# A wait for VectorE in front of each GpSimd operation on their shared port

## The chip, the core and the metric

The kernel runs on one NeuronCore of a Trainium2 chip. The core has five engines that run side by side, each through its own instruction queue in program order: TensorE (PE in the profile, its weight loads PEld), VectorE (DVE), ScalarE (ACT), GpSimd (POOL) and SyncE (SP), which here only starts DMA transfers. Engines wait for one another through semaphores. TensorE reads SBUF and writes PSUM; VectorE and ScalarE reach both memories; GpSimd works on SBUF alone. The metric is the device time of one launch in microseconds (us), lower being better.

## The reference

Eight batches, twelve heads, 448 tokens, head size 64. Attention uses a sigmoid in place of a softmax; its output, with the heads side by side, is the input of a gated linear layer whose gate is a causal convolution of five taps.

```python
scores = scale * np.matmul(q, k.transpose(0, 1, 3, 2)) - np.log(S)
attn = 1.0 / (1.0 + np.exp(-scores))
x = np.matmul(attn, v)                    # then (B, S, 768)
for k in range(5):
    gate_pre += conv_w[k][None, None, :] * xp[:, k:k + S, :]
gate = 1.0 / (1.0 + np.exp(-gate_pre))
out = gate * (x @ w_val) @ w_out
```

## The kernel before, in words

All results must be good to float32, so most operands are split in two: a high part in a narrow type and a low part, which is the source minus the high part. Three matmuls (high by high, low by high, high by low) then stand for one.

*Attention.* Heads are taken in 48 pairs. A pair's q and k arrive in one tile `qk_src` [128, 896]. Two copies (L387 on VectorE or L385 on ScalarE) make `qk_hi`, two subtractions on GpSimd make `qk_lo` (`split_qk`, through the helper `sub`, L396). Scores go to PSUM (`scores`, L560; the leftover rows L583), ScalarE takes the sigmoid (L596) and the scaled high part `a` (L391), VectorE the low part (`a`, `a_rest`, L607, read from PSUM). The product with v (`v_hi`, L393, and `v_lo`, L627) is L646 and L654. The first pairs run as plain float32 without splits.

*Gate.* The attention output `x` is scaled and split into `xs` (L393 high, L785 low). The taps are multiplied on ScalarE or VectorE (L391, L393, L723) and some are summed by DMAs that GpSimd issues and that add into `gate` (L727). ScalarE takes the sigmoid (L729).

*The two linear layers.* `product("val")` multiplies `xs` by the weights (L984), VectorE joins the gate (L994, L1004). For the later batches the second layer is done with one level of a fast matrix product: `mix` makes sums and differences of weight blocks (`mix`, `mixed`; L396, L806, L812, L814, L823), `form` makes sums of blocks of the gated values (four additions in place, L861, then high and low parts, L387 and L396), and `product_mixed` runs the smaller products (L921) and collects them in `y` (L934).

*Order.* Every operation is an `Op` with a list of engines that may do it, the tiles it reads and writes, and a mark `port`: the default `"VG"` says that it uses the SBUF port shared by VectorE and GpSimd when it runs on either; `port=""` says that it does not (operations that read PSUM, reductions, memsets, and the DMAs that GpSimd issues). The table `ORDER` lists all 2724 operations in one sequence, the string `ENGINES` gives one letter to each (P, V, A, G or S). `plan.issue()` reads the two and the last loop emits the operations in that sequence, so each engine's queue holds its own operations in the order of the table. Between engines only data and buffers make anyone wait: nothing in the kernel before holds a GpSimd operation until a VectorE operation that stands ahead of it in the table has run, unless it reads or overwrites a tile of that operation.

On GpSimd the table puts 97 operations with the port mark (60 subtractions for `qk_lo`, the rest in `mix`, `form` and two for `g`), 60 DMA issues and 24 memsets without it.

Of the kernel before, what the change touches and what calls it, by code (L numbers as in the profile page):

```python
# [278 lines left out]
def attention_then_gate(  # L279
# [20 lines left out]
    nc = tc.nc  # L300
# [755 lines left out]
    def rest(j):  # L1056
        o = scores_rest(j)
        t = tau(2 * j) + AT["a_rest_first" if 2 * j < AHEAD else "a_rest"]
        two[j]["a_next"] = lambda: attention(two[j], t, two[j]["ps"], rest_ring, "a_rest", j in WHOLE)
        return o  # L1060
# [5 lines left out]
    for j in range(TWOS):  # L1066
# [10 lines left out]
        else:  # L1077
            o = rest(j + 1) if j + 1 < TWOS else None
# [49 lines left out]
    product_mixed(B - 2, range(NQ - HELD, NQ), AT["held"])  # L1128
    product_mixed(B - 1)
    plan.close(rings)  # L1130
    for o in plan.issue():
        o.emit(o.eng)


# [47 lines left out]
```

## Time and profile before

| | |
|---|---|
| time, median of 3 runs | 587.87 us (587.75 to 588.45) |
| the profiled execution | 586.95 us, its span 585.1 us |
| TensorE busy | 564.8 us, 97% of the span |
| VectorE busy | 502.0 us, 86% |
| ScalarE busy | 453.7 us, 78% |
| GpSimd busy | 187.8 us, 32% (208 instructions) |
| chain of waits, by engine | PE 63%, DVE 27%, ACT 5% |

The span runs from the first to the last instruction; the time has some 1.9 us around it. A busy TensorE is not TensorE at its peak, since matmuls overlap and their ends are modelled. The chain of waits is followed back from the last instruction, at each step to what released it.

### The profile page before, as it was taken

To read this page: it belongs to the slowest core of one execution; us is meant where nothing else is said; L and a number is where in the kernel's file an instruction comes from. 1 tells how busy PE (TensorE), PEld (TensorE's weight loads), DVE (VectorE), ACT (ScalarE), POOL (GpSimd) and SP (SyncE) were. 2 spreads that over 40 slices of the span, in tenths; PEclk is the share of its full clock that TensorE was granted. 3 is DMA by queue.
4 is the path that set the end of the run, shared out by engine and by line. 5 is a ranking of instruction groups with operands and counts; after the bars stand their busy time and mean duration, and the time that the engine had idled before them with its cause. 6 is when DMAs were issued, how large, how long until landed. Compare 5 with 4: busy or idle time off the path is not lost.

```text
span 585.1 us, 10537 instructions
## 1 busy us (share of the span) xinstructions
PE 564.8 (97%) x4043; PEld 323.5 (55%) x4043; DVE 502.0 (86%) x814; ACT 453.7 (78%) x609; POOL 187.8 (32%) x208
## 2 busy tenths in 40 slices
PE   9999999899989898899999999999999999999996
PEld 4343334344544456565557754467655775456685
DVE  2778999999999999998999999998789886994633
ACT  5688687797979998898999997998958987673220
POOL 0000122534527544325672412432323313112410
PEclk9999999999999999999999999999999999999999
DMA  8689767936364645667555754667755454535114
GB/s 323 266 256 320 279 138 173 241 57 176 77 162 105 152 123 107 180 151 180 134 147 119 195 122 110 158 146 162 176 138 127 118 120 105 109 72 109 37 37 145
DMA packets 40081, 88.50 MB, mean 151 GB/s; under 512 B 14944, under 2 KB 21216, under 8 KB 40032
## 3 DMA queue, kind: packets, MB, share of 16 engines
q1 hardware_dynamic: 31392, 56.37, 29.4%
q0 software_dynamic: 8640, 31.46, 28.7%
q8 instruction: 32, 0.52, 0.4%
q14 instruction: 17, 0.14, 0.1%
HBM read 43.96 MB, written 12.40 MB: 96 GB/s over the span
## 4 chain that ended last, share of the span: by engine, by line
PE 63%; DVE 27%; ACT 5%; issue 2%; DMA 1%; ACTq 0%; DVEq 0%
PE ps_m L984 17%; PE ps_m L921 12%; PE ps_a L654 11%; PE ps_a L560 11%; PE ps_a L921 7%; DVE a L607 5%; PE ps_a L583 2%; DVE gate L723 2%; PE ps_a L646 2%; ACT ps_a L596 2%; DVE v_lo L627 1%; DVE gate L994 1%; DVE xs L393 1%; DVE xs L785 1%; DVE w_words L419 1%
## 5 line engine op out<-in xcount | busy, mean ns | idle before, releaser
L984 PE MATMUL ps_m<-xs,w_val_hi 128*128 128x512 f16 x504 | 150.9, 381 | 0.0
L596 ACT ACTIVATE ps_a<-ps_a 128x896 f32<-128x896 f32 x112 | 100.1, 906 | 23.0 <-PE ps_a L560 7.3
L727 POOL DMA_DIRECT2D gate<-tap x60 | 53.2, 887 | 182.3 <-ACT tap L391 90.0
L607 DVE SCALAR_TENSOR_TENSOR a<-ps_a,a 128x896 f16<-128x896 f32 x96 | 102.4, 1081 | 9.1 <-ACT a L391 8.2
L984 PE MATMUL ps_m<-xs,w_val_lo 128*128 128x512 f16 x252 | 95.8, 380 | 0.0
L396 POOL TENSOR_TENSOR qk_lo<-qk_src,qk_hi 128x448 fp32r<-128x448 f32 (+1 forms) x60 | 72.0, 1224 | 62.8 <-DVE qk_hi L387 26.8
L391 ACT ACTIVATE a<-ps_a 128x896 f16<-128x896 f32 x96 | 86.9, 916 | 1.0
L391 ACT ACTIVATE tap<-x,cw 128x512 f32<-128x512 f32 x120 | 84.6, 723 | 1.1 <-DVE x L705 1.1
L984 PEld LDWEIGHTS <-w_val_hi 128*128 128x128 f16 x504 | 47.9, 98 | 57.2 <-issue 7.7
L921 PEld LDWEIGHTS <-mixed 128*128 128x128 f16 x648 | 62.4, 98 | 17.6 <-issue 6.9
L921 PE MATMUL ps_m<-form,mixed 128*128 128x256 f16 x432 | 60.0, 273 | 2.9 <-DVE y L934 2.6
L654 PE MATMUL ps_a<-a,v_hi 128*64 128x448 f16 x384 | 52.7, 355 | 0.0
L596 ACT ACTIVATE a_single<-ps_a 128x896 f32<-128x896 f32 x56 | 47.2, 926 | 4.7 <-PE ps_a L560 4.1
L560 PE MATMUL ps_a<-qk_single 64*128 64x448 f32 x216 | 45.4, 562 | 0.0
L560 PE MATMUL ps_a<-qk_hi 64*128 64x448 f32 x180 | 38.4, 422 | 4.7 <-DVE a_rest L607 2.4
L921 PE MATMUL ps_m<-form,w_out_hi 128*128 128x256 f16 x216 | 39.7, 273 | 2.2 <-DVE y L934 1.5
L984 PEld LDWEIGHTS <-w_val_lo 128*128 128x128 f16 x252 | 24.8, 98 | 30.1 <-issue 0.6
L921 PEld LDWEIGHTS <-w_out_hi 128*128 128x128 f16 x324 | 30.3, 98 | 14.8 <-issue 8.6
L654 PE MATMUL ps_a<-a_single,v_src 128*64 128x448 f32 x192 | 37.8, 543 | 0.0
L723 DVE SCALAR_TENSOR_TENSOR gate<-x,cw,gate 128x512 f32<-128x512 f32 x48 | 36.1, 764 | 0.1
L654 PE MATMUL ps_a<-a,v_lo 128*64 128x448 f16 x192 | 34.2, 352 | 0.0
L560 PE MATMUL ps_a<-qk_lo,qk_hi 64*128 64x448 f32 x180 | 33.4, 365 | 0.0
(170 smaller groups left out, 1053.8 us busy)
## 6 DMA issues: line engine op xcount, KB each, us to landing
gate<-tap POOLq DMA_DIRECT2D x60, 512.0 KB, 4.7
qk_src<-qk SPq DMA_DIRECT2D x30, 448.0 KB, 3.7
v_src<-vs SPq DMA_DIRECT2D x24, 448.0 KB, 4.6
out_t<-y SPq DMA_DIRECT2D x36, 224.0 KB, 3.6
qk_single<-qk SPq DMA_DIRECT2D x17, 448.0 KB, 6.2
w_words<-w_val SPq DMA_DIRECT2D x6, 768.0 KB, 5.8
w_words<-w_out SPq DMA_DIRECT2D x6, 768.0 KB, 5.0
x<-first_x SPq DMA_DIRECT2D x21, 68.0 KB, 4.0
```

The costliest lines, as they stand in the source:

```text
L391: nc.scalar.activation(to, x, AF.Copy, scale=by)
L396: engines[eng].tensor_tensor(to, x, y, op=ALU.subtract)
L560: mm(b()[:, h, :S], k()[rows, at : at + P], q()[rows, :S], start=(n == 0), stop=(n == len(terms(i)) - 1))
L583: mm(b()[to, h, :S], x[n]()[rows, CW:], x[n]()[rows, :S], start=True, stop=True)
L596: nc.scalar.activation(to, b()[:, :, :S], AF.Sigmoid, bias=-math.log(S), scale=1.0 / math.sqrt(D))
L607: op({"V": 1.0}, t + 0.5, lambda e: nc.vector.scalar_tensor_tensor(part(1), p(), A_SCALE, part(0), op0=ALU.mult, op1=ALU.subtract), [b], [ ...
L646: mm(px()[to, p, :S], v()[rows, h * D : (h + 1) * D], x(s["a"])[rows, h, at : at + S], start=(j > 0 and n == 0), stop=(j == 0 and n == len ...
L654: mm(px()[to, p, :S], v()[:, o : o + D], x(st[2 * j + p]["a", c])[:, h, at : at + S], start=(j == 0 and c == 0 and n == 0), stop=(j > 0 an ...
L723: op({"V": 0.67}, at + AT["tap_step"] * k + AT["tap_pair"] * p, lambda e, p=p, part=part, k=k: nc.vector.scalar_tensor_tensor(part(), x()[ ...
L727: op({"G": 1.1}, at + AT["tap_step"] * k, lambda e, tap=tap: nc.gpsimd.dma_start(g(), tap(), accum_op=ALU.add), [tap], [g], 4 * P * T * 4, "")
L921: mm(to(), stat[a](), src()[:, f, :], start=(first and c == 0 and j == 0), stop=(c == NQ - 1 and j == 2), skip_group_check=True)
L984: mm(po()[:, cs], w()[:, c, :], x(k)[:, cs], start=(c == 0 and j == 0), stop=(c == NC - 1 and j == 2))
```

## The change

While the operations are emitted, the loop remembers the last instruction of the latest VectorE operation that has the port mark (`shared`). The first instruction of each GpSimd operation with the mark gets a dependency on it, with a semaphore. The 60 DMA issues and the memsets get none; nor does VectorE ever wait for GpSimd by it. Where an operation has several instructions (the four additions of `form`), only the first one gets the wait. Nothing else changes.

```diff
     plan.close(rings)
+    shared, kinds = None, {"V": mybir.EngineType.DVE, "G": mybir.EngineType.Pool}
+    in_turn = mybir.DependencyInfo(mybir.DependencyClass.Sync, mybir.DependencyReason.DATA)
     for o in plan.issue():
+        made = nc.cur_bb.bb.instructions
+        seen = len(made)
         o.emit(o.eng)
+        if o.eng in kinds and o.eng in o.port:
+            mine = [i for i in made[seen:] if i.engine == kinds[o.eng]]
+            if o.eng == "V":
+                shared = mine[-1]
+            elif shared is not None:
+                tc.add_manual_dep(mine[0], shared.name, in_turn, reason="the shared port, in turn")
```

## Rows read from the trace of the kernel before

**Rows 1.** Five longest waits of PE, 105 to 300 us: waiter <- releaser: us, times, longest.
```profile
PE ps_m L921 <- DVE y L934: 4.1, 3, 2.6
PE ps_a L580 <- DVE a L607: 2.9, 2, 2.4
PE ps_a L560 <- DVE a_rest L607: 2.4, 1, 2.4
PE ps_a L560 <- DVE a L607: 1.8, 2, 1.5
PE ps_a L646 <- DVE a L607: 0.7, 1, 0.7
```

**Rows 2.** Windows: stretch, length, busy us of each engine, PEclk, DMA share, GB/s.
```profile
105.00:244.00 139.00, 126.80 (x898) 68.16 (x896) 135.60 (x206) 123.04 (x167) 66.74 (x68) 0.99 0.56 134
115.00:119.50 4.50, 4.26 (x18) 2.17 (x19) 4.50 (x5) 3.32 (x5) 1.59 (x2) 0.62 0.72 161
141.00:160.00 19.00, 19.00 (x121) 10.14 (x118) 17.63 (x33) 18.26 (x27) 8.08 (x10) 1.00 0.54 134
300.00:540.00 240.00, 238.98 (x1813) 147.08 (x1810) 207.69 (x341) 198.12 (x267) 72.01 (x76) 1.00 0.57 132
```

**Rows 3.** Timeline, 157.5 to 166 us: start us, us, instruction [idle before <-releaser].
```profile
158.83 4.40 DVE L393 TENSOR_SCALAR xs<-x,x_exp 128x1024 f16<-128x1024 f32 x1
159.33 3.34 POOL L396 TENSOR_TENSOR qk_lo<-qk_src,qk_hi 128x384 fp32r<-128x384 f32 x3
163.15 1.27 DVE L785 SCALAR_TENSOR_TENSOR xs<-x,x_exp,xs 128x1024 f16<-128x1024 f32 x1
164.35 2.07 DVE L607 SCALAR_TENSOR_TENSOR a<-ps_a,a 128x896 f16<-128x896 f32 x2
165.48 0.18 PE L580 MATMUL ps_a<-vm,ones 128*128 128x1 bf16 x1 [2.44 <-DVE a L607]
```

**Rows 4.** DVE groups by form, 105 to 250 us: count | busy us, mean ns.
```profile
L393 DVE TENSOR_SCALAR xs<-x,x_exp 128x1024 f16<-128x1024 f32 x3 | 5.9, 1961 | 0.0
L393 DVE TENSOR_SCALAR v_hi<-v_src,v_exp 128x896 f16<-128x896 f32 x2 | 4.7, 2330 | 0.0
```

**Rows 5.** The same forms, 320 to 540 us.
```profile
L393 DVE TENSOR_SCALAR xs<-x,x_exp 128x1024 f16<-128x1024 f32 x4 | 3.0, 746 | 0.0
L393 DVE TENSOR_SCALAR v_hi<-v_src,v_exp 128x896 f16<-128x896 f32 x4 | 2.7, 677 | 0.0
```

**Rows 6.** Timeline of DVE, 105 to 118 us: two operations of one form.
```profile
107.69 2.78 DVE L814 TENSOR_TENSOR mix<-mix,w_out_lo 128x384 f32<-128x384 f32 x1
...
112.49 0.56 DVE L814 TENSOR_TENSOR mix<-mix,w_out_lo 128x384 f32<-128x384 f32 x1
```

**Rows 7.** Timelines at the first and the last late GpSimd operation.
```profile
71.90 1.28 DVE L471 TENSOR_SCALAR out_inverse<-out_inverse 128x2 f32<-128x2 f32 x1
71.94 1.21 POOL L396 TENSOR_TENSOR mix<-mix,w_out_lo 128x384 f32<-128x384 f32 x1
483.98 0.88 DVE L387 CAST qk_hi<-qk_src 128x384 fp32r<-128x384 f32 x1
483.51 1.13 POOL L396 TENSOR_TENSOR qk_lo<-qk_src,qk_hi 128x448 fp32r<-128x448 f32 x1 [2.00 <-issue]
```

**Rows 8.** Timelines, 246 to 248 us: a GpSimd operation right behind the VectorE one it reads.
```profile
246.52 0.38 DVE L387 CAST qk_hi<-qk_src 128x448 fp32r<-128x448 f32 x1
247.03 1.14 POOL L396 TENSOR_TENSOR qk_lo<-qk_src,qk_hi 128x448 fp32r<-128x448 f32 x1 [5.96 <-PE ps_a L560]
```

**Rows 9.** Timelines, 301 to 309 us: the additions of `form`, what they run beside, what follows.
```profile
301.29 1.22 DVE L396 TENSOR_TENSOR form<-gate,form 128x1024 f16<-128x1024 f32 x1
302.42 1.08 DVE L607 SCALAR_TENSOR_TENSOR a_rest<-ps_a,a_rest 128x896 f16<-128x896 f32 x1
301.33 4.17 POOL L861 TENSOR_TENSOR gate<-gate 128x256 f32<-128x256 f32 x4 [2.47 <-DVE form L396]
306.27 1.23 DVE L396 TENSOR_TENSOR form<-gate,form 128x1024 f16<-128x1024 f32 x1
```

## The prediction

> **What bounds the kernel now.** I read five views in this order: the engines' sums, the waits of TensorE, the windows, the costliest groups by form, the timeline of VectorE and GpSimd together.
>
> TensorE is the bound, and it is nearly full: from 300 to 540 us it is busy 238.98 of 240 us [rows 2], so nothing can be won there. What it loses it loses between 105 and 300 us, and there it waits for VectorE: 4.1 + 2.9 + 2.4 + 1.8 + 0.7 = 11.9 us in the five longest rows [rows 1]. In the same stretch, 105 to 244 us, VectorE is busy 135.60 of 139 us, ScalarE 123.04 and TensorE 126.80 [rows 2]. So VectorE is the local bound there, and the question is whether its work is real.
>
> Part of it is not. Set the same instruction side by side. `xs` (L393) takes 0.746 us between 320 and 540 us [rows 5], but 1.961 us on average between 105 and 250 us [rows 4]; `v_hi` takes 0.677 us against 2.330 us. The timeline shows what stretches them: the `xs` at 158.83 us lasts 4.40 us while three GpSimd subtractions of together 3.34 us run inside it [rows 3], and a `mix` of 0.56 us lasts 2.78 us at 107.69 [rows 6]. An operation without the port mark is not touched: `a_rest` at 302.42 takes 1.08 us beside a GpSimd addition [rows 9], as much as two `a` with none beside them (2.07 us, rows 3).
>
> I then counted each VectorE operation's time over the middle time of its form without GpSimd beside it. The excess is about 30.8 us in all. The order table says whose doing it is: 24.5 us fall on operations that only met GpSimd operations standing behind them in the table, which had run ahead; 3.1 us on operations that met only earlier ones; the rest is mixed. The first and the last with a later one beside it are at 71.90 and 483.98 us [rows 7]; with these two they are 20.
>
> **What the change does, part by part.**
>
> *The wait itself.* Of the 97 GpSimd operations with the mark, 48 already start after the VectorE operation that they would now wait for; nothing changes for them. The other 49 start before it has ended, the first at 71.94 and the last at 483.51 us [rows 7]; these are held, by 110.5 us added up over all 49 (0.1 to 8.7 us each, against the VectorE times of before). The release is cheap: the subtraction at 247.03 starts 0.13 us behind the copy that it reads, which ends at 246.90 [rows 8].
>
> *VectorE.* The 24.5 us of excess go where the culprit is held. In exchange the held operations meet whatever VectorE does next. In the table a marked operation stands directly behind the awaited one in 1 case of 97, and in none of the 49; mostly an `a` follows, which reads PSUM and is not touched. What an operation in its turn costs is seen in the 48: 3.1 us of excess, 0.06 us each. For 49 more that is 3 us. Net on VectorE: 24.5 - 3 = 21.5 us, most of it between 71 and 250 us. The bounds: 0, if every held operation finds another victim, and 28, if the mixed cases go too.
>
> *What of it reaches the end.* VectorE's time counts only where TensorE waits for it. The large single cases stand just ahead of such waits: `xs` (3 x (1.961 - 0.746) = 3.6 us, rows 4 and 5), of which 3.65 us is the one at 158.83, ahead of the wait of 2.44 us at 165.48 [rows 3]; `v_hi` (2 x (2.330 - 0.677) = 3.3 us), ahead of the 2.6 us of `y` [rows 1]; `mix` (2.78 - 0.56 = 2.2 us, rows 6), ahead of the 2.4 us of `a_rest`. In each the excess is about as large as the wait or larger. So the 11.9 us can go almost whole. Beside them stands the clock: it is at 0.62 between 115 and 119.5 us [rows 2], a mix of 1.2 and 2.4 GHz, just after the wait of 2.4 us for `a_rest`; if that wait goes, I count 1.0 us back (between 0 and 4.5 x 0.38 = 1.7). Ceiling: 12.9 us.
>
> *What is late next.* ScalarE. Its 123.04 us of work between 105 and 244 us [rows 2] would have to fit in 139 - 12 = 127 us. Its fullest stretch is 18.26 of 19 us, 96% [rows 2]; at that share 123.04 us need 128.0 us, which leaves 11.0 us of gain. I take 10.8 us.
>
> *What the held operations cost.* Their readers: `qk_lo` is read by score matmuls mostly 3 to 20 us after it is made, so a hold of 1 to 5 us is covered. The subtractions at 159.33 wait for the `xs` low part at 163.15, which itself comes 3.65 us sooner and would end at 160.8; three subtractions of 1.0 to 1.1 us then end near 164.1. The first, which the scores behind the matmul at 165.48 want, is done by 162.1 [rows 3]. The tightest place is `form`: the four additions at 301.33 would wait for the operation at 301.29, until 302.5, and VectorE's work on their result (the last piece at 306.27, rows 9) is used by TensorE 0.6 us after it ends. Held by 1.2 us, they cost TensorE 0.6 us if they still take 4.17 us, and less if part of the 4.17 us was the first one's own waiting beside that operation, as the start 0.04 us behind it suggests. I take 0.4 us for all such places, 0 to 2 as bounds.
>
> *The queue behind.* GpSimd's queue runs in order, so a held operation also holds the DMA issues and memsets behind it. GpSimd is idle two thirds of the time, and the next DMA of the same sum mostly waits for a landing or a ScalarE product anyway; with 1 to 2 us of hold I count nothing. If that cover went, a gate would come 1 to 2 us late, once per batch at most.
>
> Sum, in the profiled execution: 586.95 - 10.8 + 0.4 = 576.6 us. The median of before lies 0.9 us above that execution, so 577.5 us.
>
> **The rivals.**
>
> *ScalarE takes over earlier.* If it keeps a share of 92% instead of 96% between 105 and 244 us, 123.04 us of work need 133.7 us: 5.3 us gained, 582.6 us. For it: ScalarE is close to full. Against it: much of its idle time there is spent on VectorE's results, which come sooner.
>
> *Contention only moves, and the holds bite: slower.* The place is the port right after the awaited operation: if the next marked VectorE operation takes it before the released GpSimd operation does, or is caught by it, VectorE wins nothing, while the holds stay. The subtractions at 159.33 then wait until 164.4 and end 3.3 us later, at 167.7, 2.2 us after the matmul at 165.48; the additions of `form` cost 0.6 us more. That is +2.8, 590.7 us. It decides when most of the held operations meet a marked one directly behind; the table has this once in 97. The Trainium skill speaks for this rival: its page "SBUF — State Buffer", section "SBUF: two separate sides", calls the shared pair an exclusive lock that the one who comes first keeps for the whole instruction while the other fully blocks. By that rule a GpSimd operation released at the end of one VectorE operation competes with the next, and waiting only changes the victim. The trace agrees on the blocking (4.40 us around 3.34 us, rows 3).
>
> *The wait never acts*, because another one already implies it or it is not put in: 587.9 us. Against it: 49 operations demonstrably start early.
>
> **How the numbers follow.** The forecast 0.70, with its own range 573.6 to 581; ScalarE's case 0.15 (581 to 586.5); no effect 0.05; slower 0.10. About 0.2% (1.2 us) is what a measurement of this kernel can tell from no change. Faster: 0.70 + 0.14 = 0.84; the same: 0.05 + 0.01 = 0.06; slower: 0.10. The lower end, 573.5, is the median less 11.9, the clock's upper bound of 1.7 and 0.8 us of two shorter waits that rows 1 leave out; the upper end, 585.5, takes in most of ScalarE's case.
>
> **What would show it.** Right: between 105 and 250 us `xs` and `v_hi` fall to 0.75 and 0.68 us; VectorE's busy time falls by about 20 us to some 482; GpSimd's own falls too; the waits of TensorE for VectorE shrink to 2 us or less and the clock at 115 us stays at 1.00. Wrong in the step on ScalarE: TensorE's rows then name ScalarE (`x`, `a`, `y`). Wrong in the step on the holds: TensorE waits for `qk_lo` or `form` on GpSimd, or VectorE for the additions of `form`. The prediction falls as a whole if the groups of VectorE keep their stretched means.

## The result, and the profile after

The changed kernel takes 569.1 us (median of 4 runs, 568.12 to 569.96), the kernel before 587.81 us in the same session (586.65 to 588.45): ratio 0.9683, 95% interval 0.9661 to 0.9705. The direction and the main cause were as forecast, but the gain is 18.7 us, and 569.1 lies below the range's lower end of 573.5. From profiled execution to profiled execution it is 586.95 to 569.2 us, 17.75, where the sum had 10.4. All profiled executions below ran at a granted clock of 0.994 or more but that of `apart_25` (0.945), from which only durations on VectorE are taken.

The engines' sums of the changed kernel: busy us, share of its span of 567.4 us, instructions.

```profile
PE 560.7 (99%) x4043; PEld 322.6 (57%) x4043; DVE 478.2 (84%) x814; ACT 452.6 (80%) x609; POOL 180.2 (32%) x208
```

VectorE lost 23.8 us of busy time with the same 814 instructions, GpSimd 7.6 us with the same 208. TensorE was at 97% and is at 99%.

All waits of TensorE in the changed kernel, whole span: waiter <- releaser: us, times, longest.

```profile
PE ps_m L1027 <- DVE ones L1020: 1.1, 1, 1.1
PE ps_a L560 <- DMA qk_single<-qk: 0.4, 1, 0.4
PE ps_a L560 <- DVE a L607: 0.3, 1, 0.3
```

All five rows of [rows 1] are gone from their stretch. The first row here is the start of the kernel (1.09 us), and before had it too; the last one stands at 367 us.

Windows of the changed kernel, columns as in [rows 2]. The work of 105 to 244 us of before now ends at 228 us.

```profile
105.00:244.00 139.00, 139.00 (x1047) 78.91 (x1045) 133.06 (x228) 133.48 (x183) 68.49 (x73) 1.00 0.61 150
105.00:228.00 123.00, 123.00 (x895) 67.41 (x892) 117.65 (x206) 118.69 (x163) 61.31 (x66) 1.00 0.62 149
228.00:284.00 56.00, 56.00 (x427) 32.84 (x425) 52.02 (x85) 52.65 (x71) 28.85 (x33) 1.00 0.60 147
112.50:116.00 3.50, 3.50 (x24) 2.04 (x23) 3.50 (x6) 3.50 (x5) 1.85 (x3) 1.00 0.15 19
```

In the first row TensorE is busy for all 139 us (126.80 before) and its clock is at 1.00, also in the stretch of the last row, which takes in what answers to 115 to 119.5 us of before, then at 0.62.

VectorE by form, 105 to 250 us: count | busy us, mean ns.

```profile
L393 DVE TENSOR_SCALAR xs<-x,x_exp 128x1024 f16<-128x1024 f32 x3 | 2.2, 746 | 0.0
L393 DVE TENSOR_SCALAR v_hi<-v_src,v_exp 128x896 f16<-128x896 f32 x3 | 2.0, 682 | 0.0
```

The means of 1961 and 2330 ns [rows 4] have become 746 and 682, the plain values of [rows 5].

Timelines of the changed kernel: start us, us, instruction [idle before <-releaser]. First what answers to the stretched `mix` of [rows 6], then the stretch of [rows 3].

```profile
107.04 0.55 DVE L814 TENSOR_TENSOR mix<-mix,w_out_lo 128x384 f32<-128x384 f32 x1
...
152.52 0.75 DVE L393 TENSOR_SCALAR xs<-x,x_exp 128x1024 f16<-128x1024 f32 x1
153.18 1.28 DVE L785 SCALAR_TENSOR_TENSOR xs<-x,x_exp,xs 128x1024 f16<-128x1024 f32 x1
154.38 3.08 DVE L607 SCALAR_TENSOR_TENSOR a<-ps_a,a 128x896 f16<-128x896 f32 x3
154.55 3.04 POOL L396 TENSOR_TENSOR qk_lo<-qk_src,qk_hi 128x384 fp32r<-128x384 f32 x3 [1.16 <-DVE xs L785]
156.34 0.38 PE L984 MATMUL ps_m<-g,w_out_lo 128*128 128x512 f16 x1
156.56 0.17 PE L580 MATMUL ps_a<-vm,ones 128*128 128x1 bf16 x1
```

The `xs` takes 0.75 us in place of 4.40; the three subtractions wait 1.16 us for its low part and run beside three unmarked `a`, which take 3.08 us as they would alone. The L580 matmul follows its neighbour without the wait of 2.44 us.

*Where the 17.7 us of span came from.* TensorE runs the same instructions in the same order in both kernels. So for each I compared the time from the start of the one in front to its own start, in both traces. The differences: 112 to 119 us of before 4.09 (2.50 of a wait, 1.59 of slower matmuls behind it), 133 to 139 us 1.96, 165 us 2.60, 182 and 192 us 0.59, 200 us 1.61, 223 to 229 us 1.68, 244 us 2.67, 298 us 0.75, after 300 us 1.16 (four places with 1.50, one that lost 0.34), and before 105 us 0.35. Sum 17.5.

### The profile page after: what moved, and what is told of

Its sections match the earlier page's. It is cut to its first block, busy times and chain, and to the rows that moved or that the text cites. A ratio compares the mean times of both kernels' runs of the same rounds, so it can differ in the third digit from the quotient of the medians.

```text
span 567.4 us, 10556 instructions
## 1 busy us (share of the span) xinstructions
PE 560.7 (99%) x4043; PEld 322.6 (57%) x4043; DVE 478.2 (84%) x814; ACT 452.6 (80%) x609; POOL 180.2 (32%) x208
## 4 chain that ended last, share of the span: by engine, by line
PE 94%; DVE 2%; DMA 1%; POOL 1%; issue 1%; ACT 1%; SPq 0%; DVEq 0%
PE ps_m L984 32%; PE ps_a L560 18%; PE ps_a L654 16%; PE ps_m L921 15%; PE ps_a L921 7%; PE ps_a L583 4%; PE ps_a L646 3%; DMA qk_single<-qk 1%; POOL gate L861 1%; DVE a L607 0%; DVE form L396 0%; DVE gate L861 0%; DVE gate L994 0%; DVE xs L785 0%; DVE form L387 0%
## 5 line engine op out<-in xcount | busy, mean ns | idle before, releaser
L727 POOL DMA_DIRECT2D gate<-tap x60 | 54.6, 910 | 164.4 <-ACT tap L391 86.3
L396 POOL TENSOR_TENSOR qk_lo<-qk_src,qk_hi 128x448 fp32r<-128x448 f32 (+1 forms) x60 | 65.9, 1110 | 72.5 <-DVE qk_hi L387 23.6
L391 ACT ACTIVATE a<-ps_a 128x896 f16<-128x896 f32 x96 | 86.9, 916 | 1.0
L391 ACT ACTIVATE tap<-x,cw 128x512 f32<-128x512 f32 x120 | 84.7, 725 | 1.1 <-DVE x L705 1.1
```

The lines of the kernel that those rows point to most:

```text
L391: nc.scalar.activation(to, x, AF.Copy, scale=by)
L396: engines[eng].tensor_tensor(to, x, y, op=ALU.subtract)
L727: op({"G": 1.1}, at + AT["tap_step"] * k, lambda e, tap=tap: nc.gpsimd.dma_start(g(), tap(), accum_op=ALU.add), [tap], [g], 4 * P * T * 4, "")
```

## The experiments

Each kernel was timed against the kernel before on the same chip. Diffs are against the changed kernel. "Excess" is VectorE's time over the middle time of each form, counted from the profiled execution as in the prediction. The count gives 31.0 us for before (30.8 in the prediction) and 8.0 for the change.

| kernel | us (before) | ratio, 95% interval | excess us |
|---|---|---|---|
| the change | 569.1 (587.8) | 0.968 [0.966, 0.971] | 8.0 |
| late_only | 569.0 (588.2) | 0.968 [0.965, 0.972] | 7.9 |
| rest_only | 587.9 (588.2) | 1.000 [0.998, 1.002] | 31.2 |
| nine | 576.6 (588.2) | 0.980 [0.976, 0.985] | 22.1 |
| before_300 | 570.7 (588.2) | 0.971 [0.967, 0.974] | 12.5 |
| one_early | 570.1 (586.7) | 0.972 [0.968, 0.976] | 9.9 |
| op_before | 569.6 (587.8) | 0.969 [0.967, 0.971] | 8.6 |
| four_early | 580.7 (587.8) | 0.988 [0.986, 0.990] | 24.1 |
| heads_13 | 572.6 (587.6) | 0.973 [0.969, 0.977] | 13.1 |
| apart_25 | 586.3 (587.6) | 0.997 [0.994, 0.999] | 21.0 |
| any_op | 583.7 (586.7) | 0.993 [0.991, 0.996] | 16.3 |
| both_ways | 571.2 (586.7) | 0.973 [0.970, 0.975] | 0.4 |
| any_both | 601.9 (587.8) | 1.023 [1.021, 1.026] | 0.3 |
| act_more_5 | 571.8 (587.8) | 0.973 [0.971, 0.975] | not counted |
| act_more_16 | 581.1 (586.7) | 0.990 [0.987, 0.992] | 8.3 |

**Which waits do it: late_only and rest_only.** The 97 waits are split into the 48 operations that start too early in before and the other 49.

```diff
-    for o in plan.issue():
+    held = [292, 390, 434, 473, 481, 501, ...]      # 48 positions in the table; rest_only: the other 49
+    for at, o in enumerate(plan.issue()):
...
-            elif shared is not None:
+            elif shared is not None and at in held:
```

> The wait only on the 48 GpSimd operations that in the trace of before start ahead of the VectorE operation in front of them in the table. Theory A (order on the port: each of these, run ahead of its turn, stretches a marked VectorE operation, and TensorE waits for that): all of the gain, 568 to 571 us, xs at its 0.75 us. Rival B (pace: any hold on GpSimd and on the DMA issues behind it evens out the traffic, whichever operation is held): about half of it, near 578 us.

> The wait only on the other 49 operations, which in the trace of before already start behind that VectorE operation. Theory A: no change, 586.5 to 589 us, xs and v_hi stay stretched (means 1.96 and 2.33 us between 105 and 250 us). Rival B: about half of the gain, near 578 us.

The 48 give the whole gain, the 49 nothing. What happens is decided at operations that run out of turn.

**Do the places add up: nine and before_300.** The same edit with `held = [473, 481, 501, 698, 703, 710, 1086, 1094, 1100]` (the nine that run inside the stretched `mix`, `xs` and `v_hi` and inside a `w_words` at 115 us) and with `held = range(1390)`, all positions up to some 300 us.

> The wait on nine operations alone, those inside the four longest stretched VectorE operations (mix at 107.69, w_words at 115.11, xs at 158.83, v_hi at 237.58 us). Theory A with prices that add up place by place: the steps of TensorE just behind them go, 4.1 (112 to 119 us, the clock with it) + 0.5 to 2.0 (133 to 139) + 2.6 (165) + 2.7 (244 us), 576.5 to 578.5 us; the steps at 200, 223 to 229 and 298 us stay. Rival C (one backlog: VectorE is nearly full, so 10.5 us taken off anywhere lets the later steps shrink too): below 575 us. Rival B: 9 of 97 holds, under 2 us gained.

> The wait on all marked GpSimd operations among the first 1390 of the table, which run before 300 us. Theory A: TensorE's steps before 300 us go (16.6 us), the small ones after it stay (1.1 us): 570 to 571.5 us. Rival B: the holds are spread over the whole kernel, 61 of 97 fall here, so some 63% of the gain, near 576 us.

With nine waits the time falls by 11.6 us, with all up to 300 us by 17.5. In the profiled execution of `nine` (577.9 us) TensorE's steps go back at the held places, by 3.66 us at 112 to 119 us, 2.71 at 165 and 2.72 at 244. At the others behind 105 us they stay within 0.3 us, but for 134 us, where 0.86 us more is lost. So the places add in the main, and removing one does not merely bring up the next. The waits behind 300 us are worth 1.7 us between the two medians, which agrees with the 1.16 us of the step count, though the two intervals overlap.

**Does the exact point of release matter: one_early, op_before, four_early.** The wait goes to the marked VectorE operation before the awaited one; to the VectorE operation of any kind directly ahead of the awaited one; to the marked operation four before it.

```diff
# one_early
-                shared = mine[-1]
-            elif shared is not None:
-                tc.add_manual_dep(mine[0], shared.name, in_turn, ...)
+                shared, ahead = mine[-1], shared
+            elif ahead is not None:
+                tc.add_manual_dep(mine[0], ahead.name, in_turn, ...)
# op_before: every VectorE operation is remembered in last
...
+                if o.eng in o.port:
+                    shared, front = mine[-1], last
+                last = mine[-1]
+            elif o.eng in o.port and front is not None:
+                tc.add_manual_dep(mine[0], front.name, in_turn, ...)
# four_early
...
+                marked.append(mine[-1])
+            elif len(marked) > 4:
+                tc.add_manual_dep(mine[0], marked[-5].name, in_turn, ...)
```

> Each marked GpSimd operation waits for the marked VectorE operation before the one it waited for, so it may start while the operation just ahead of it in the table still runs or waits. Theory A (it is the operation just ahead that suffers): a good part of the gain is lost, 574 to 584 us, with xs or v_hi or other marked forms stretched again. Rival E (any rough pacing of GpSimd behind VectorE will do): 569 to 571 us.

> Each marked GpSimd operation waits for the VectorE operation that stands directly in front of the marked one that it waited for in the change: a shorter hold than the change's, but let go just where a marked operation begins. Theory G (what counts is what VectorE does next when GpSimd is let go; the two runs that waited for an end of a marked operation kept the gain, the one that waited for an unmarked one lost most of it): the marked operation is stretched again, VectorE's time grows by 10 us or more against the change, 575 to 584 us. Rival H (what counts is only that GpSimd can't run far ahead; the loss with the wait on any operation came from holding too long): 568.5 to 571.5 us.

> Each marked GpSimd operation waits for the fifth last marked VectorE operation ahead of it in the table, so it may run up to four marked operations ahead. Theory G: it is still let go at the end of a marked operation, so most of the gain stays, 570 to 575 us, less only where the old one is long over and GpSimd starts for other reasons. Rival H: the gain shrinks with the distance, 575 to 584 us. If the old waits are mostly over before GpSimd is ready, it is the kernel before, 587 us.

I had expected `one_early` to lose much of the gain, since its released operation starts beside the one it should follow. It kept it, and so did `op_before`; `four_early` lost 11.6 us of it. The timelines say why. In `one_early` the wait is on the high part of `xs`, and the subtractions start 0.23 us into the low part:

```profile
152.49 0.98 POOL L727 DMA_DIRECT2D gate<-tap  x1 [3.94 <-ACT tap L391]
153.26 1.28 DVE L785 SCALAR_TENSOR_TENSOR xs<-x,x_exp,xs 128x1024 f16<-128x1024 f32 x1
153.49 3.97 POOL L396 TENSOR_TENSOR qk_lo<-qk_src,qk_hi 128x384 fp32r<-128x384 f32 x3
```

VectorE keeps its 1.28 us, and the first subtraction waits inside its own time: 3.97 us for three, against 3.04. `op_before` has the same 3.97 us there. In `rest_only`, where these subtractions carry no wait, the same three instructions stand in nearly the same places (the high part of `xs`, which began between them, is shown too):

```profile
158.56 0.97 POOL L727 DMA_DIRECT2D gate<-tap  x1 [3.96 <-DVE qk_hi L387]
158.65 0.75 DVE L393 TENSOR_SCALAR xs<-x,x_exp 128x1024 f16<-128x1024 f32 x1
159.32 4.38 DVE L785 SCALAR_TENSOR_TENSOR xs<-x,x_exp,xs 128x1024 f16<-128x1024 f32 x1
159.54 3.06 POOL L396 TENSOR_TENSOR qk_lo<-qk_src,qk_hi 128x384 fp32r<-128x384 f32 x3
```

Again the subtractions are recorded 0.22 us behind VectorE's operation, yet now VectorE loses 3.1 us. In `four_early` the wait is there but long fulfilled, and the `xs` is as long as in before:

```profile
152.51 0.88 POOL L727 DMA_DIRECT2D gate<-tap  x1 [3.95 <-DVE qk_hi L387]
152.62 4.39 DVE L393 TENSOR_SCALAR xs<-x,x_exp 128x1024 f16<-128x1024 f32 x1
153.12 3.33 POOL L396 TENSOR_TENSOR qk_lo<-qk_src,qk_hi 128x384 fp32r<-128x384 f32 x3
```

So the order of the recorded starts does not tell who has the port. A wait that is still open when VectorE's operation begins does.

**Who takes the port without a wait: heads_13 and apart_25.** With that I went back to the trace of before and took each place in which a GpSimd operation is recorded inside a marked VectorE operation that began first. Where GpSimd had been idle for 0.1 us or more ahead of it (16 places, without one whose VectorE operation had met another subtraction before), VectorE lost 0.02 us at most. Where it stood right behind a DMA issue that began before VectorE's operation (9 places), VectorE lost 1.1 to 3.7 us in seven. In the two others it lost nothing. In one the issue had begun 0.06 us ahead only. In the other, at 282.25 us, the subtraction reads a copy that VectorE ended 0.01 us after the operation at 282.25 had begun, so its wait was still open. (The rest stand behind a GpSimd computation or a memset and tell nothing apart.) Before's timelines, one place of each kind and then the one at 282.25 us ([rows 3] have the VectorE side of the first):

```profile
158.72 0.88 POOL L727 DMA_DIRECT2D gate<-tap  x1 [3.93 <-DVE qk_hi L387]
...
185.03 1.15 DVE L627 SCALAR_TENSOR_TENSOR v_lo<-v_src,v_exp,v_hi 128x896 f16<-128x896 f32 x1
185.21 2.37 POOL L861 TENSOR_TENSOR gate<-gate 128x256 f32<-128x256 f32 x2 [1.00 <-DVE form L396]
...
281.60 1.08 POOL L727 DMA_DIRECT2D gate<-tap  x1
281.88 0.38 DVE L387 CAST qk_hi<-qk_src 128x448 fp32r<-128x448 f32 x1
282.25 0.35 DVE L387 CAST qk_hi<-qk_src 128x384 fp32r<-128x384 f32 x1
282.41 1.44 POOL L396 TENSOR_TENSOR qk_lo<-qk_src,qk_hi 128x448 fp32r<-128x448 f32 x1
```

The DMA issue at 158.72 begins 0.11 us before the `xs` at 158.83, and the subtractions behind it win. The additions at 185.21 start out of idle, and `v_lo` keeps its plain 1.15 us. Two kernels divide the 48 late operations by this: `heads_13` holds the 13 that are recorded right behind a DMA issue or a memset, `apart_25` the 25 that start out of idle or behind one that does; the 10 left out are queued behind one of the 13. The edit is that of `late_only` with other lists.

> The wait is kept for 13 of the 48 late GpSimd operations: those recorded right behind another GpSimd instruction of another kind (a DMA issue or a memset) with no idle time between. Theory K: a GpSimd operation that waits for no semaphore has the port from the start of the instruction in front of it, so a VectorE operation recorded first still loses. In the trace of before such operations, with those recorded behind them without a gap, go with 20.4 of the 24.5 us of excess. Their places on TensorE in the change are 112-119 us (4.09), 133-139 (1.96), 165 (2.60), 223-229 (1.68), 244 (2.67) and 409 (about 0.3): 13.3 us, so 574.5, between 573 and 576.5; VectorE's excess some 10. Rival Q: being out of turn is what costs, on each of the 48 alike: 13/48 of 18.6 us is 5.0, so 582.8, above 580.

> The wait is kept for 25 other late operations: those that start out of an idle GpSimd, or behind one that does. Theory K: where GpSimd starts out of idle time inside a VectorE operation, VectorE keeps the port and GpSimd waits (185.03 us in before: the 1.15 us operation keeps its 1.15 us, the first addition takes about 1.6 us in place of 0.8), so most of these waits win nothing; left are the places at 182-192 us (0.6), 200 (1.61), 298 (0.75) and 0.5 after 300: 3.5 us, so 584.3, between 583 and 586; the xs at 159 us stays above 4 us. Rival Q: 25/48 of 18.6 us is 9.7, so 578.1, below 580.5.

Thirteen waits give 15.0 us between the medians (13.4 to 18.4 by the interval), twenty-five others 2.0 by the ratio (0.6 to 3.4). So being out of turn is not by itself what costs. `heads_13` fell a little below its range, since the small steps at 182, 192 and 412 us went too. That it is the issue or memset in front that makes the difference rests on comparing places: the 13 were chosen from the trace that also shows who lost, and no run moves an issue away from its place. In its trace the stretch of [rows 3] looks as in the change:

```profile
152.57 1.28 DVE L785 SCALAR_TENSOR_TENSOR xs<-x,x_exp,xs 128x1024 f16<-128x1024 f32 x1
153.93 3.06 POOL L396 TENSOR_TENSOR qk_lo<-qk_src,qk_hi 128x384 fp32r<-128x384 f32 x3 [1.16 <-DVE xs L785]
```

In `apart_25` the low part of `xs` is at 4.26 us. It loses a third of the excess and hardly any time; much of what remains, this `xs` among it, lies ahead of TensorE's waits.

**Later than its turn: any_op.** GpSimd waits for the last VectorE operation of any kind, marked or not.

```diff
-        if o.eng in kinds and o.eng in o.port:
+        if o.eng in kinds:
...
-            elif shared is not None:
+            elif o.eng in o.port and shared is not None:
```

> Each marked GpSimd operation waits for the latest VectorE operation of any kind ahead of it in the table, the unmarked ones (which read PSUM or reduce) included. This holds GpSimd longer, mostly by one operation of 1.1 us. Theory A: nothing to win on the port beyond the change, and the readers of GpSimd's results have the slack: 568 to 572 us. Rival D (the holds are at the edge of what the readers bear): TensorE waits for qk_lo or form, 573 us or more.

I expected about the time of the change and measured 583.7 us: a miss. The waits of TensorE in `any_op`:

```profile
PE ps_a L560 <- DVE a L607: 5.1, 7, 1.8
PE ps_m L921 <- DVE form L396: 1.1, 3, 0.5
...
PE ps_m L921 <- POOL x L700: 0.9, 1, 0.9
```

And one place in its timeline:

```profile
212.49 2.12 POOL L396 TENSOR_TENSOR form<-gate,form 128x1024 f16<-128x1024 f32 x1 [3.78 <-DVE x_max L702]
213.03 1.88 DVE L387 CAST qk_hi<-qk_src 128x448 fp32r<-128x448 f32 x1
```

Held for 3.78 us behind a reduction that does not use the port, the subtraction comes out beside the next marked operations and costs a copy of 0.38 us 1.5 us. 15.7 of the excess of 16.3 us come from GpSimd operations that stand ahead of their victim in the table. This is the prediction's slower rival, contention that moves while the holds bite, made real by a wait on the wrong operations. It took most of the gain, not all.

**Order on both sides: both_ways and any_both.** Now a marked VectorE operation also waits for the GpSimd operation ahead of it; `any_both` adds this to `any_op`.

```diff
             if o.eng == "V":
                 shared = mine[-1]
+                if taken is not None:
+                    tc.add_manual_dep(mine[0], taken.name, in_turn, ...)
+                    taken = None
-            elif shared is not None:
+            else:
+                taken = mine[-1]
+                if shared is not None:
...
```

> Besides the wait of the change, each marked VectorE operation also waits for the marked GpSimd operation ahead of it in the table. Theory A: with GpSimd in turn, the next marked VectorE operation comes 2 to 3 us later, so most of these waits are already over; VectorE's idle time grows by a few us, the time stays within 569 to 573 us. Rival F (the order table does not fit the real durations): VectorE idles behind GpSimd at many places and the time rises above 575 us.

> GpSimd waits for the latest VectorE operation of any kind, as in the run that lost most of the gain, and each marked VectorE operation waits for the marked GpSimd operation ahead of it, so the two never meet on the port and only the holds are left. If that run lost by collisions (theory G), VectorE's operations are at their plain times again, but VectorE now waits the same time in the queue: 577 to 585 us, with 10 us or more of VectorE idle behind GpSimd. If it lost because GpSimd's results came too late for TensorE (rival H), TensorE waits for qk_lo or form on GpSimd and VectorE's waits are short: also 577 to 585 us. The row that tells is who VectorE and TensorE wait for; both_ways had TensorE wait 0.2 us for anything of GpSimd's.

The excess goes to 0.4 us, yet `both_ways` is some 2 us slower than the change (the two intervals just touch): VectorE now waits where it was stretched, 15.9 us in all for GpSimd (2.0 in the change). So the change's remaining 8.0 us of excess can't be had in this way. `any_both` has next to no excess and is the one kernel slower than before, 601.9 us where 577 to 585 had been expected: a miss. VectorE waits 50.4 us for GpSimd there, which costs more than meeting on the port did. TensorE's waits there:

```profile
PE ps_a L560 <- DVE a L607: 11.2, 9, 2.4
PE ps_a L560 <- DVE a_rest L607: 3.6, 4, 1.3
```

**How near ScalarE is: act_more_16 and act_more_5.** In the change 16, or 5, of the scaled copies `a` (L391) between 120 and 233 us of before are done twice, the same values again: 14.7 and 4.6 us more work for ScalarE.

```diff
+    again = [497, 629, 779, 914, 1039]
+    for at, o in enumerate(plan.issue()):
...
         o.emit(o.eng)
+        if at in again:
+            o.emit(o.eng)
```

> The change, with 16 of ScalarE's operations a (L391, 0.92 us each) between 105 and 228 us issued twice, 14.7 us more work, the same values written again. It tests the step of the prediction that went wrong, ScalarE at 96% as the next bound. If ScalarE is that bound, nearly all of it shows: TensorE then waits for a or x on ScalarE, 578 to 583 us. If its queue only runs behind and catches up after 228 us, a third or less shows: below 574 us.

> The change, with 5 of ScalarE's operations a between 105 and 228 us issued twice (4.6 us more work). 16 of them (14.7 us) cost 12.0 us. If ScalarE has a fixed margin of 14.7 - 12.0 = 2.7 us and then bounds, it costs 1.9 us: 571 us. If every operation costs the same share, 82%: 3.8 us, 572.9 us. If the margin is larger than 4.6 us, nothing: 569 us.

14.7 us cost 12.0 us and 4.6 cost 2.7, against the change's 569.1. ScalarE is close to being the bound, with a margin of some 2 us (14.7 - 12.0 and 4.6 - 2.7); whether the margin is fixed or each addition costs its share the two runs can't settle. In `act_more_16`, first TensorE's wait rows, then the window that answers to before's 105 to 244 us:

```profile
PE ps_a L560 <- DVE a L607: 5.8, 6, 1.8
PE ps_m L921 <- ACT y L391: 1.1, 1, 1.1
```

```profile
105.00:240.00 135.00, 126.70 (x897) 68.20 (x896) 118.78 (x206) 132.45 (x179) 61.30 (x66) 0.99 0.57 136
```

ScalarE is busy 98% there, VectorE 88%, and VectorE stands between: the row names `a` on VectorE, which itself waits for ScalarE's `a`.

No kernel here beats the change measurably; with TensorE at 99% little is left for one.

## Why the prediction was right in direction and wrong in size

*Right.* VectorE was the local bound by time that was not work, the wait acts, the held operations are late in few places, and no other VectorE operation became the victim in their stead: busy time of VectorE fell by 23.8 us (21.5 in the sum) and the means fell to 746 and 682 ns, as forecast. The rival in which the wait never acts and the one in which contention moves are out for this kernel.

*Wrong: the step "What of it reaches the end".* It priced the loss by the five wait rows, 11.9 us. Start to start, the same stretches had lost 13.6 us, 0.6 of it in two small steps beside the rows (134 and 182 us). The timeline of before shows where such a difference comes from (the matmul ahead of the 2.44 us wait of [rows 3]):

```profile
162.66 0.38 PE L984 MATMUL ps_m<-g,w_out_lo 128*128 128x512 f16 x1
```

From its start to that of the L580 matmul at 165.48 are 2.82 us; in the change they are 0.22 (156.34 to 156.56). That is 2.60 won, where the row said 2.44, as idle time is counted only from the modelled end of the matmul. Then the clock: counted at 1.0, it gave 1.59, near the upper bound of 1.7. Before's windows show where the clock was low:

```profile
113.00:115.20 2.20, 0.00 (x0) 0.00 (x0) 2.20 (x5) 2.12 (x4) 0.69 (x2) 1.00 1.04 377
116.00:119.00 3.00, 3.00 (x13) 1.31 (x10) 3.00 (x4) 1.82 (x3) 0.59 (x1) 0.50 0.87 165
```

TensorE did nothing for the 2.2 us of the first row and afterwards ran at 0.50, the lower level of 1.2 GHz. Behind the waits at 165 and 244 us, of about that length, its clock stayed at 1.00, so the price of a wait on the clock can't be read from the wait alone.

*Wrong: the first step, "from 300 to 540 us ... nothing can be won there".* 1.16 us were won behind 300 us and 0.35 before 105 us. With 0.75 at 298 us, a wait that the prediction put into its range and not into its sum, that makes 2.26 left out. Several of these steps are too short to have a wait row of their own, and a TensorE that is 99.6% busy by modelled ends hid them.

*Wrong: the step "What is late next".* It cut the ceiling of 12.9 to 10.8 because all 123.04 us of ScalarE's work had to fit at a share of 96%. The share was right: 133.48 of 139 us is 96%. The demand was not: TensorE passed the same instruction with ScalarE having done 118.69 us in the window to 228 us, 4.35 less than before. From there to 284 us it was busy 52.65 of 56 us, 94%, and made 3.5 of this up. The stretch of before that answers to it, where ScalarE had 49.17 us:

```profile
244.00:299.80 55.80, 55.21 (x419) 32.23 (x417) 52.59 (x84) 49.17 (x67) 28.35 (x30) 1.00 0.60 147
```

So part of ScalarE's work was ahead of its readers and could come later. That cut of 2.1 us did not happen.

*Wrong, small: "What the held operations cost".* 0.4 us were counted for them and no wait row of TensorE names `qk_lo` or `form`: nothing. That they are 48 and not 49 changed nothing; the forty-ninth started 0.05 us after its operation had ended.

From 10.4: + 1.7 (rows, and the two steps beside them), + 0.6 (clock), + 2.3 (places left out), + 2.1 (ScalarE), + 0.4 (holds) = 17.5, against 17.75 measured. The remaining 0.9 us of the 18.7 is what the sum put between the profiled execution of before and its median.

*Right result, reason too coarse: "The wait itself".* The prediction held all late operations alike, by the order table. `heads_13` shows that the ones queued behind a DMA issue or memset carry most of the gain, and the first trace already had the two kinds side by side.

## What to carry to other kernels

Where two engines share a port, look for operations whose time grows beside the other engine's, and see what stands in the other's queue in front of the culprit: an operation with no open wait, queued behind a DMA issue, is the one to hold, and a wait on its turn, or on the operation just before it, was enough here; holding it longer gave most of the gain back. Price what a bound engine loses by comparing start-to-start times with the same instructions at full pace, not by adding its idle rows, and count the short steps too. An engine at 96% is a bound only if its work can't be put off beyond the stretch.

## What the runs showed of the hardware that I had not expected

A GpSimd operation can win the port from a VectorE operation that is recorded ahead of it. The Trainium skill, "SBUF — State Buffer", section "SBUF: two separate sides", gives the shared pair to whichever starts first, for the whole instruction, while the other fully blocks. The trace agrees where GpSimd starts out of idle (185.03 us in before) or had its wait still open (153.26 in `one_early`, 282.25 in before). By the recorded starts it does not agree where the GpSimd operation stands behind a DMA issue without an open wait: at 159.32 us in `rest_only` VectorE was recorded first by 0.22 us and lost 3.1 us. That such an operation claims the port about when the issue in front of it begins fits the places above: VectorE operations that began 0.11 us behind the issue lost 3.65 us (158.83 us in before, 152.62 in `four_early`), and those at 0.06 us (130.47 in before) and 0.09 us (158.65 in `rest_only`) lost nothing. It was not measured by itself; that GpSimd's start behind an issue is only recorded late would look the same.

Nor does the blocked VectorE operation get in between operations queued in a row: it waited for three, 4.40 us for 0.75 [rows 3]. In the changed kernel the largest excess left is again behind a DMA issue, at an operation in its turn:

```profile
92.00 0.86 POOL L727 DMA_DIRECT2D gate<-tap  x1 [1.31 <-ACT tap L391]
92.38 1.94 DVE L393 TENSOR_SCALAR gate<-x,cw 128x512 f32<-128x512 f32 x1
92.56 1.46 POOL L396 TENSOR_TENSOR qk_lo<-qk_src,qk_hi 128x448 fp32r<-128x448 f32 x1
```

The tap product with 0.48 us of its own takes 1.94 us, though it is recorded 0.18 us ahead of the subtraction.
